# Decay rows of the float32 score tiles issued from GpSimd's queue, and another issue order

## The chip, the cores and the metric

The kernel runs on one core of a Trainium2 chip. The metric is the device time of one execution in microseconds (us). Three runs of the kernel before took 1042.11, 1043.04 and 1045.21 us; their median, 1043.04 us, is the time that the change is measured against. One further execution was profiled; it took 1040.97 us, and the first and the last instruction in its trace are 1039.0 us apart (its span).

## The reference: what is computed

Eight batches of eight heads, each with 576 positions of 64 values, go through causal attention with a decay, and the result (4608 tokens of 512 values) through two matrix products with a cosine between them.

```python
scores = scale * np.matmul(q, k.transpose(0, 1, 3, 2))
log_f = np.log(np.clip(f, 0.0001, 1.0))
cum = np.cumsum(log_f, axis=-1)
decay = cum[:, :, :, None] - cum[:, :, None, :]
scores = np.where(causal, -1000000000.0, scores + decay)
...                                   # softmax over the last axis, then times v
h = x @ w_in
g = h * np.cos(h)
return (g @ w_out).astype(np.float32)
```

The decay is a difference of two numbers, one of the row and one of the column. The kernel lays `cum` as an extra row beside the 64 rows of q and another beside those of k (with constants as partners), so the matmul that makes the scores adds the decay as well.

## The kernel before, in words

**Tiling.** Heads are taken in pairs, so there are 32 pairs, four to a batch. Each head's scores are five blocks of 128 rows, cut at the diagonal, in three PSUM tiles: one with 576 columns (`pa2`), one with 448 and 64, and one with 320 and 192 (both `pa1`). The first four pairs (`N32 = 4`) run `attention32`: scores in float32 (line 697, two products of 288 columns for the 576), exponentials on ScalarE (line 715), transposes on TensorE (line 668) with evacuations (lines 656, 657), products with v (line 742), a division by the sums (755, 756, 758), transposes (765) and a split into two float16 halves (769, 771). Pairs 4 to 7 still make float32 scores (line 865) from the same kind of tile, but go on like the rest: softmax (879, 884, 889, 892), halves of the probabilities (901, 905), a transpose by DMA (910), products with v (934). Pairs 8 to 31 use split scores (867, 868).

**The float32 tiles.** Pairs 0 to 7 (`NQ = 8`) use four tiles `Q`, one for each head of two pairs in turn. `load32` fills one: 64 partitions of q and k by a 288 KB transfer (line 636, on SyncE's queue, SP), and two decay rows of 576 numbers (2.2 KB each, line 640), one to partition 64 and one to partition 65. The rows come from SBUF (`cm`, shown as `vv`, since it lies in that buffer) in the first batch and from a copy in DRAM (`cum_d`) in the second. A tile's rows can only be written when the score matmuls of the tile's user before are done. Pair 0 (`NACT = 1`) issues its four rows from ScalarE's queue.

**The weights.** Both weight matrices come in as 64-bit words. VectorE makes float32 of them (483, 487, 491), ScalarE takes a bound by a sum of squares (502), a largest value over all partitions is found by `allmax` (a diagonal tile `dg` made on VectorE at line 434 or on GpSimd at line 438, a matmul at line 441, a maximum at line 443), GpSimd makes a power of two of it (424, 425), and the weights are split in float16 halves (512, 519, or 516 and 517 on GpSimd). A raw block waits for its place in a ring of three (`h`) or eight (`g`).

**The MoE part.** `gemm1` (line 964) and `gemm2` (line 1010), each by three float16 products for one float32 product; the cosine stage lies between them (970 to 994).

**The order.** Every piece of work is an operation with a number, recorded in program order. The string `ORDER` lists these numbers in the order in which all engines' instructions are issued; each engine works through its own part of it in sequence, and waits where its next instruction's inputs are not there. An "a" behind a number takes the operation's other form (a piece of work that VectorE and GpSimd can both do, say). "+44" behind a number puts 44 filler matmuls (line 1077, 448 columns, results never read) on TensorE ahead of that operation.

```python
for pads, fill, fn in seq:
    for _ in range(pads):
        T.matmul(fill(), ones, mask[:, 0:PAD], start=True, stop=True)
    fn()
```

Of the kernel before, what the change touches and what calls it, by code (L numbers as in the profile page):

```python
# [43 lines left out]
N32, NQ, NACT = 4, 8, 1  # L44
# [27 lines left out]
796 586a 786 601 604 813 787 597 797 818 542 799 617 605 798 819 602 773 598 800 820 618+1 801 607 814 802 606 949 821 619 803 948 825 804  # L72
620 774 621 599 822 837 805 622 826 623 608 624 806 658 600 625 807 641 662+1 827 626 828 838 659 642 808 678 627 839 643 609 676+1 823 628
679 644 663 629 664+2 809 677 630 645 810 829 631 646 811 830 660 840 831 632 832 610 672 665 661 633 841 877+1 634 673 647 674+1 878 635
648a 824 833 611 834 858+3 933 836 842 636 714 879 843 637 859 649 692 638 844 835 650 675 845 639 698 612 893 651 984 860 640 865 652 693
666 880 861 862 667 613 699 653 846 614 668 694 654 700 847 848 655 669 863 889 657 670 680 681 715 986 710 947 656 682 864 695 881 866 1438
701 867 683 868 882 869 696 883 895 870 671a 871 884 697 885 926 712 872 886 873 887 684 874 849 1148 890 876 875 896 702 902 853 891 927
914 897 903 850 716 898 711 1022 851 945 904 915 713 899 726 916 905 888 717 906 718 917 730 727 907 728 731 985 908 918 719 1026 900 919
1029 854a 969 909 703 920 901 729 724 910 921 911 922 720 913 912 950 970 923 686 685a 951 924 971 972 957 1027a 704 958 925 959 952 721 687
973 953 725 954 974 1031 960 955 975 732 1021 994 961 928 956 962 1082 963 733 964 965 976 987 966 977 734 995 1083 968 1032 978 705 996 967  # L80
979 997 735 941 929 1006 998 980 1445 999 688 1007 1023 1008 1000 988 1009 689 1010 1229 989 1028 1001 706 690 1011 990 1002 1012 691 991
1013 1003 1030 1014 946 1273 722 707 1015 992 723a 1004 1016 942 981 993 1017 736 934 943 737 1230a 1084 982 708 983 709 1085 1234a 1231
1033 1005 1018 1034 935 936a 1235 1040 1019 1086 1020 1052 1041 937 1068 1274a 1053 938 1054 1042 1055 1278a 1275 1070 1035 1276 1956 1043
1232 1036 1037 1069 939 1072 940 1056 1038 1071 1044 1074 1073 1045 1446 1046 1024 1057 1058 1279 1124 1314 1075 1047 1277 1076 1233 1270
1077 1126 1125 1048 1059 1039 1078 1122 1957 1025 1064 1049 1127 1060 1120 1061 1065 1050 1079 1243 1121 1062 1123 1236 1271 1128 1140 1080
1066 1129 1255 1100 1318 1315 1081 1051 1130 1134 1320a 1237 1238 1131 1101 1102 1244 1132 1087 1239 1319a 1256 1317 1245 1240 1103 1063
1257 1141 1246 1133a 1241 1287 1258 1138 1242 1259 1316 1288 1104 1247 1289 1280 1248 1290 1260 1249 1136 1250 1281 1135 1251 1291 1252 1139
1108 1292 1447a 1137 1665 1254 1142 1261 1143 1110 1262 1282 1109 1283 1263 1284 1253 1112 1144 1293 1584 1264 1272 1355 1299 1358 1265 1106
1266 1111 1145 1294 1113 1151 1285 1300 1107 1114 1155 1115 1359a 1105 1153 1156 1152 1286 1149 1154 1301 1116 1363 1360 1321 1458 1302 1448
1117 1088 1267 1295 1150 1296 1118 1094 1364 1298 1297 1303 1157 1268 1089 1304 1305 1449 1306 1158 1146 1090 1307 1147a 1159 1308 1340 1399  # L90
1309 1095 1341 1342 1322 1311 1269 1323 1119 1328 1091 1403 1329 1400 1324 1361 1160 1310 1096 1404a 1092 1312 1325 1450 1326 1313 1330 1207
# [150 lines left out]
T_DGE = 0.5  # L242
# [79 lines left out]
def fox_moe_kernel(ctx: ExitStack, tc: tile.TileContext, qkT, vp, fT, w1, w2, out):  # L322
    nc = tc.nc
    V, A, G, T = nc.vector, nc.scalar, nc.gpsimd, nc.tensor
    dma = nc.sync.dma_start
# [37 lines left out]
    ks = slice(64, 64 + S)  # L363
# [744 lines left out]
```

## Time and profile before

| | |
|---|---|
| median of three runs | 1043.04 us |
| the profiled execution | 1040.97 us |
| its span | 1039.0 us |
| TensorE busy in the span | 1027.0 us (99%) |
| VectorE, ScalarE, GpSimd busy | 774.9, 789.5, 294.8 us |
| granted TensorE clock | 1.000 |
| filler matmuls | 99 |
| decay-row transfers issued by SP, by ScalarE | 28, 4 |

A busy TensorE here is one that executes matmuls, the fillers among them. The engines' shares over the whole span hide that the kernel has two stages: about the first 100 us, in which weights are read and converted and the first pairs are worked off, and the rest, in which the two matrix products dominate. The prediction reads them apart.

### The profile page before, as it was taken

What the parts mean: (1) busy time and instruction counts of PE and PEld (TensorE: products, weight loads), DVE (VectorE), ACT (ScalarE), POOL (GpSimd) and SP (SyncE); (2) the same over time, 40 slices, a digit from 0 to 9 for tenths busy, and PEclk for the clock granted to TensorE, in tenths of its full rate; (3) what the DMA queues carried; (4) which work ended last, traced back from release to release, by engine and by line L of the source; (5) the groups of instructions that cost most, each with busy time, mean ns of one, the idle gap of its engine ahead of it and who ended that gap; (6) DMA issues with size and microseconds to landing.
All of it is one profiled execution on the core that took longest, in us unless ns stands there. A gap on an engine that the chain in (4) does not pass through costs nothing. (4 is left out here: it accounts for less than half of the span.)

```text
span 1039.0 us, 23384 instructions
## 1 busy us (share of the span) xinstructions
PE 1027.0 (99%) x8915; PEld 831.6 (80%) x8916; DVE 774.9 (75%) x1710; ACT 789.5 (76%) x1711; POOL 294.8 (28%) x381
## 2 busy tenths in 40 slices
PE   8999999999999999999999999999999999999998
PEld 4788777778888877888778877888778877888787
DVE  8999998778678676787877688586877967663531
ACT  5999999788768797898877789686878877753431
POOL 3223213432341343332332424233141313300110
PEclk9999999999999999999999999999999999999999
DMA  8997525856685757668465766947466583520001
GB/s 261 288 321 200 130 55 128 185 107 162 154 175 147 163 132 163 139 144 183 114 145 135 176 142 159 193 83 164 124 170 136 121 189 56 122 39 16 7 14 34
DMA packets 255920, 144.77 MB, mean 139 GB/s; under 512 B 223736, under 2 KB 231928, under 8 KB 255808
## 3 DMA queue, kind: packets, MB, share of 16 engines
q1 hardware_dynamic: 255680, 143.27, 58.4%
q8 instruction: 70, 1.15, 0.4%
q14 instruction: 42, 0.34, 0.1%
q10 hardware_dynamic: 128, 0.01, 0.0%
HBM read 71.41 MB, written 9.68 MB: 78 GB/s over the span
## 5 line engine op out<-in xcount | busy, mean ns | idle before, releaser
L1010 PE MATMUL hp<-g,W2s 128*128 128x320 f16 (+1 forms) x3072 | 391.8, 286 | 0.2
L964 PE MATMUL hp<-xh,W1s 128*128 128x320 f16 (+1 forms) x2048 | 381.3, 286 | 1.5 <-ACT h L970 1.4
L964 PEld LDWEIGHTS <-W1s 128*128 128x128 f16 x3072 | 295.5, 98 | 78.6 <-issue 1.8
L1010 PEld LDWEIGHTS <-W2s 128*128 128x128 f16 x3072 | 296.3, 98 | 76.1 <-issue 0.6
L964 PE MATMUL hp<-xl,W1s 128*128 128x256 f16 (+1 forms) x1024 | 292.6, 286 | 0.0
L905 DVE SCALAR_TENSOR_TENSOR PS<-pa,ri,PS 128x576 f16<-128x576 f32 (+3 forms) x280 | 146.1, 544 | 57.3 <-ACT PS L901 55.9
L884 ACT ACTIVATE pa<-pa,nb 128x576 f32<-128x576 f32 (+4 forms) x280 | 141.5, 506 | 48.5 <-DVE nb L879 43.1
L901 ACT ACTIVATE PS<-pa,ri 128x576 f16<-128x576 f32 (+3 forms) x280 | 137.7, 531 | 31.1 <-DVE ri L892 27.0
L889 POOL TENSOR_SCALAR ri<-L 128x1 f32<-128x1 f32 (+1 forms) x168 | 53.9, 321 | 352.0 <-ACT pa L884 347.1
L879 DVE CUSTOM_DVE_ANT_0 pa<-pa,mask 128x576 f32<-128x576 f32 (+4 forms) x280 | 134.7, 500 | 24.0 <-PE pa L868 20.4
L970 ACT ACTIVATE h<-hp 128x320 f32<-128x320 f32 (+1 forms) x256 | 100.1, 411 | 36.5 <-PE hp L964 32.8
L994 POOL TENSOR_TENSOR g<-h,g 128x1024 f16<-128x1024 f32 (+1 forms) x32 | 83.5, 2609 | 149.0 <-ACT g L992 147.3
L985 DVE TENSOR_TENSOR h<-h,r 128x1280 f32<-128x1280 f32 (+1 forms) x64 | 89.6, 1399 | 34.4 <-ACT r L983 33.9
L983 ACT ACTIVATE r<-r,halfpi,m_inv 128x1280 f32<-128x1280 f32 (+1 forms) x64 | 86.2, 1348 | 31.2 <-DVE r L981 29.0
L981 DVE SCALAR_TENSOR_TENSOR r<-r,m_b,h 128x1280 f32<-128x1280 int32 (+1 forms) x64 | 93.6, 1462 | 1.1
L867 PE MATMUL pa<-Q 128*128 128x288 f32 (+4 forms) x288 | 90.4, 327 | 1.2 <-DVE PS L905 0.7
L979 DVE TENSOR_SCALAR r<-h,m_a 128x1280 int32<-128x1280 f32 (+1 forms) x64 | 54.9, 858 | 44.9 <-ACT h L970 43.0
L992 ACT CAST g<-h 128x1280 f16<-128x1280 f32 (+1 forms) x64 | 73.8, 1154 | 10.6 <-DVE h L985 10.4
L934 PEld LDWEIGHTS <-vv 128*64 128x64 f16 x1512 | 68.6, 110 | 10.3 <-issue 9.5
L868 PE MATMUL pa<-Q 68*128 68x288 f32 (+4 forms) x288 | 76.6, 304 | 0.0
L934 PE MATMUL pa<-pt,vv 128*64 128x256 f16 (+2 forms) x1512 | 76.6, 254 | 0.0
L1016 ACT ACTIVATE ot<-hp,m_o 128x320 f32<-128x320 f32 (+1 forms) x64 | 32.2, 503 | 47.6 <-PE hp L1010 36.2
(127 smaller groups left out, 1182.5 us busy)
## 6 DMA issues: line engine op xcount, KB each, us to landing
stage<-in_dram SPq DMA_DIRECT2D x48, 576.0 KB
stage<-in_dram SPq DMA_DIRECT2D x32, 320.0 KB
v<-in_dram SPq DMA_DIRECT2D x32, 320.0 KB
h<-in_dram SPq DMA_DIRECT2D x16, 512.0 KB
g<-in_dram SPq DMA_DIRECT2D x16, 512.0 KB
Q<-Q SPq DMA_DIRECT2D x48, 144.0 KB
out_dram<-ot SPq DMA_DIRECT2D x32, 160.0 KB
Q<-in_dram SPq DMA_DIRECT2D x16, 288.0 KB
```

The costliest lines, as they stand in the source:

```text
L867: T.matmul(c, hi[:, 0, isl], hi[:, 1, d], start=True, stop=False)
L879: op("DVE", c_dve(w) + 0.008, lambda view=view, ib=ib, o=o, w=w, mk=mk, c=c: V.tensor_tensor_reduce(out=view(ib, o, w), in0=view(ib, o, w) ...
L884: op("ACT", c_act(w, True, 2), lambda view=view, ib=ib, o=o, w=w, c=c: A.activation(view(ib, o, w), view(ib, o, w), AF.Exp, bias=nb.get()[ ...
L901: op("ACT", c_act(w, True, 1), lambda view=view, ib=ib, o=o, w=w, c=c, out_=out_: A.activation(out_(0), view(ib, o, w), AF.Copy, scale=ri. ...
L905: op("DVE", c_dve(w) + 0.06, lambda view=view, ib=ib, o=o, w=w, c=c, out_=out_: V.scalar_tensor_tensor(out_(1), view(ib, o, w), ri.get()[: ...
L934: T.matmul(d, vv.get()[:, jb, hd, kv], m, start=first and x == 0, stop=last and x == 2)
L964: T.matmul(hp.get()[:, 0:w_], WS_[1][:, at(1, 4 * c + cb), w, fs], x.get(), start=(n == 0), stop=(n == 11))
L970: op("ACT", c_act(w_, True), lambda hp=hp, k=k: A.activation(h.get()[:, k, 0:w_], hp.get()[:, 0:w_], AF.Copy, scale=float(2.0 ** -24)), re ...
L981: op("DVE", c_dve(N) + 0.045, lambda: V.scalar_tensor_tensor(fl(r), fl(r).bitcast(I32), b1.get()[:, c:c + 1], fl(h), op0=ALU.mult, op1=ALU ...
L983: op("ACT", c_act(N, aps=2), lambda: A.activation(fl(r), fl(r), AF.Sin, scale=inv.get()[:, c:c + 1], bias=halfpi), reads=[inv], writes=[r] ...
L985: op("DVE", c_dve(N), lambda: V.tensor_tensor(fl(h), fl(h), fl(r), op=ALU.mult), reads=[r], writes=hk, prio=pr)
L1010: T.matmul(po.get()[:, 0:w_], WS_[2][:, at(2, 4 * c + k), w, msl], gh.get()[:, i, k, 0:w_], start=(n == 0), stop=(n == 47))
```

## The change

The decay rows of pairs 1 to 7 (28 transfers) are issued by GpSimd in place of SP; pair 0's stay with ScalarE. The string `ORDER` is another from its first line on, and with it the choice of forms ("a" stands 104 times, before 118 times) and the fillers (110, before 99).

```diff
 ORDER = """
-0 50 60 55 70 25 1 2 4 51 27 52 26 72 61 71 53 62 54 63 3 65 11 56 192 57 95 64 100 6 58 125 7a 170 33+44 28 34 35 40+1 66 37 29 36 67 12
+0 11 50 55 60 95 25 1 2 4 26 125 51 3 52 124 6 7 27 192 56 53 57 54 58 12 65 70 61 72 59 62 96 71 170 63 97 64 33+53 175 100 40 9 34 105 66
 ...
         for k, r in ((1, 64), (0, 65)):
-            op(*(("SP", T_DGE) if n >= NACT else ("ACT", 0.35)), lambda k=k, r=r: (dma if n >= NACT else A.dma_start)(t[r:r + 1, k, ks], src()),
+            op(*(("POOL", 1.0) if n >= NACT else ("ACT", 0.35)), lambda k=k, r=r: (G.dma_start if n >= NACT else A.dma_start)(t[r:r + 1, k, ks], src()),
                reads=[CF if b > 0 else cm], writes=[q.part(1 + k)], prio=pr, size=DMC // 4)
```

The numbers beside an engine's name (0.5 as `T_DGE`, 0.35, 1.0) are planning costs in us; the order in the string was laid out by them, and nothing in the running program reads them.

**GpSimd, after its opening memsets.** Here stand GpSimd's next twelve rows before: the decay's small remainder (line 462), then the steps of `allmax` (409 clamps a maximum, 438 makes the diagonal tile), of the scale (424, 425) and of the sums (755).

```order
L462 TENSOR_TENSOR g<-vv,g 64x576
L409 TENSOR_SCALAR m_w<-m_w 128x1
L424 TENSOR_SCALAR s_109<-u_w 128x1
L425 TENSOR_SCALAR r_110<-u_w 128x1
L755 TENSOR_SCALAR ri<-L 128x2x3
L755 TENSOR_SCALAR ri<-L 128x2x2
L409 TENSOR_SCALAR vm_427<-vm_427 128x1
L438 TENSOR_SCALAR dg<-eye,vm_427 128x128
L409 TENSOR_SCALAR m_w<-m_w 128x1
L424 TENSOR_SCALAR vs<-vu 128x1
L425 TENSOR_SCALAR vr<-vu 128x1
L438 TENSOR_SCALAR dg<-eye,m_w 128x128
```

And the same stretch of the changed kernel.

```order
L640 DMA Q<-vv 1x16x36 x3
L409 TENSOR_SCALAR m_w<-m_w 128x1
L640 DMA Q<-vv 1x16x36 x2
L424 TENSOR_SCALAR s_109<-u_w 128x1
L425 TENSOR_SCALAR r_110<-u_w 128x1
L755 TENSOR_SCALAR ri<-L 128x2x2
L640 DMA Q<-vv 1x16x36
L755 TENSOR_SCALAR ri<-L 128x2x3
L640 DMA Q<-vv 1x16x36
L409 TENSOR_SCALAR vm_435<-vm_435 128x1
L640 DMA Q<-vv 1x16x36
L438 TENSOR_SCALAR dg<-eye,vm_435 128x128
```

Decay-row transfers now stand between the small steps; line 462 is gone from GpSimd. One row further on, and in two later places, transfers stand again just ahead of a line 409 or 438.

**SP, from its first transfer.** The transfer of f (`vv`), raw weights (`h`, `g`), v for a bound (`stage`), q and k (`Q`) and, before, decay rows.

```order
L451 DMA vv<-in_dram 64x576
L493 DMA h<-in_dram 128x1024 x3
L636 DMA Q<-in_dram 64x2x576 x2
L493 DMA h<-in_dram 128x1024
L582 DMA stage<-in_dram 128x640
L640 DMA Q<-vv 1x16x36
L493 DMA g<-in_dram 128x1024 x2
L640 DMA Q<-vv 1x16x36
```

The same queue in the changed kernel.

```order
L451 DMA vv<-in_dram 64x576
L582 DMA stage<-in_dram 128x640
L493 DMA h<-in_dram 128x1024 x3
L493 DMA g<-in_dram 128x1024
L636 DMA Q<-in_dram 64x2x576
L493 DMA h<-in_dram 128x1024
L636 DMA Q<-in_dram 64x2x576
L493 DMA h<-in_dram 128x1024 x2
```

A `stage` and a `g` transfer moved ahead of the first `Q`, and a fourth `h`, which waits for its place in the ring, moved between the first and the second `Q`.

**VectorE, behind the running sum of the decay (line 455).** A piece of the difference:

```order
 L483 TENSOR_SCALAR W1s<-h 128x512
 L487 SCALAR_TENSOR_TENSOR W1s<-h,W1s 128x512
+L458 CAST g<-vv 64x576
+L460 TENSOR_TENSOR g<-vv,g 64x576
 L483 TENSOR_SCALAR W1s<-h 128x512
 L491 SCALAR_TENSOR_TENSOR W1s<-h,W1s 128x512
```

Line 458 came six rows later before, and line 460 takes the work of GpSimd's line 462.

More of the change, by code (lines that the diff above doesn't have):

```diff
@@ L72 @@
[L72 to L79, printed above, removed]
@@ new lines @@
+318 248 285 295 378 212 152 543 221 197 313 544 259 305 236 504 153 226 345 286 270 249 260 237 545a 154 203 250 291 235 319 204 446 109 113
+254 227 255 222 356 292 546 325 261 357 320 238 362 340 547 256 293 740 262 263 326 266 265 548 503 393+1 264 296 257 306 267 287 239 294
+268 297 240 300 327 359 314 329 445 328 298 230 322 307 358 242 371 335 394 321 308 315 241 333 377 299 271 386+1 404 502 395 549 372 309
+485 301 330 397 1443 302 381 334 288 387 396 303 316 323 332a 304 382 453+1 317 410 289 411 383 412a 460 228 331 388 324 454 739 384 360 461
@@ new lines @@
+770 479 581 771 795 593 582 571 591+1 588 782 594 583 572 603 592 584 783 772+1 615 595 616 604 784 796 617a 540 785 596 786 812 541 773 787
+597 601 797 799 798 542 818 1067 813 800 598 585 618 605+1 602 774 586a 599 819 801 820 619 607+2 802 620 814 621 622 803 623 658 821 624
+606 600 608 625 662 804 822 626 641 805 823 825 642 627 806 837 826 659 807 628 678 663 985 808 838 629 827 839 949 643 660 809 630 679 828
+894 810 676+1 631 644 811 948 840 632 829 664 609 645 830 661 831 657 633 646 672 677 610 832 892 841 877+1 944 665 842 647 984 634 673
@@ new lines @@
+1002 1013 707 1003 1014 737a 690 1015 942 691 1004 992 1016 981 946 1017 1084 943 982 1230 993 1085 708 1234a 709 1021 1033 1232 1018 1005
+1034 983 1040 1019 1086 1020 1052 1041 1072 1274 1445 1446 935 936 1235 1035 1279a 1068 1053 1270 1042 1276 1054 1043 1278 1055 1070 1036
+1073 1037 1314 1038 1233 1056 1074 1956 1044 1275 1069 1045 1231 1071 1057 1046 1047 937 1048 1124 1075 938 1447a 1039 939 1076 940 1064
+1024 1077 1125 1120 1271 1049 1025 1078 1051 1122 1058 1957 1126 1059 1079 1065 1060 1121 1236 1123 1050 1087 1127 1061 1140 1080 1277 1128
@@ new lines @@
+1129 1100 1141 1237 1130 1101 1062 1066 1063 1238 1243 1131 1255 1287 1244 1102 1132 1256 1239 1081a 1257 1288 1134 1315 1240 1245 1289 1290
+1316 1319 1103 1455 1246 1320a 1241 1138 1247 1242 1258 1104 1248 1358 1259 1249 1280 1291 1260 1250 1133a 1136 1281 1135 1139 1251 1282
+1252 1108 1137 1261 1254 1262 1142 1292 1263 1283 1112 1143 1293 1110 1264 1113 1284 1109 1265 1144 1253 1318 1106 1317 1266 1299 1107 1145
+1111 1151 1285 1399 1294 1155 1114 1359 1115 1152 1153 1360 1363a 1156 1286 1116 1267 1300 1301 1448 1154 1149 1449 1146 1117 1321 1302 1272
@@ new lines @@
+1464a 1499 1378 1379 1461 1177 1414 1099 1371 1162a 1380 1415 1391 1178 1381 1416 1383 1392 1356 1393 1165 1382 1417 2182 1394 1406 1425
+1407 1352 1500a 1426 1408 1427 1166 1179 1395 1409 1353 1504a 1204 1354 1428 1410 1411 1169 1418 1505a 1419 1463 1420 1501 1429 1460 1170
+1430 1180 1502 2101 1462 1421 1171 1543 1422 1746 1423 1357 1396 1431 1412 1432 1433 1434 1172 1424 1456 1435 1167 1472 1484 1473 1465 1485
+1205 1486 1544 1466 1168 1474 1467 1457 1181 1503 1436 1475 1468 1549a 1397 1487 1182 1398 1476 1488 1477 1478 1469 1489 1470 1547 1183 1173
@@ new lines @@
+1585 1559 1831 1590 1553 1796a 1554 1560 1200 1794 1588 1555 1591 1561 1225 1562 1795a 1571 1563 1611 1556 1875 1760 1586 1793 1753 1564
+1761 1592 1623 1754 1565 1572 1226 1617 1566 1755 1762 1568 1593 1612 1763 1756 1594 1764 1227 1765 1613 1573 1228 1595 1574 1618 1567 1575
+1772 1614 1835 1832 1834 1596 1792 1619 1576 1836a 1577 1757 1766 1624 1578 1620 1615 1767 1579 1773 1837a 1580 1597 1605 1774 1775 1816
+1599 1817 1787 1758 1818 1958 1616 1606 1776 1759 1819 1777 1778 1768 1779 1769 1607 1780 1820 1770 1781 1804 1782 1598 1797 1783 1621 1581
@@ new lines @@
+1682 1908 1664a 1928 1909 1910 1688 1973 1911 1943 1914 1912 1944 1930 1945 1683 1946 1931 2017a 1929 2020 1932 2021 1689 1933 1978 2019
+1974 1684 1934 1685 1935 1668 1947 1936 2022a 1948 1937 1915 1949 1693 1938 1950 2060 1951 1939 1690 1669 1694 1952 1940 1674 1953 1675 1698
+1676 1982 1941 1695 1983 1984 1677 1969 1989 2001 1678 1990 2018 1699 1691 2061a 1991 1970 2002 1992 1971 2003 1985 2062 1700 2004 2065a
+1986 2064 1987 2063 1993 1988 2005 1994 2013 1995 2006 1679 2066a 1996 1696 1997 2007 1697 1701 2008 1998 2009 2000 2014 2010 1999 2023 2011
@@ new lines @@
+3072 3073 3082 2736 3075 3074 3101 3048 3083 3120 2745 3084 2752 3121 3122 3085 3123 2738 3102 3124 2753 3086 3125 3103 2740 3087 3104 2766
+2741 2739 2746 2754 3299 3105 2747 3106 3091 3338 2767 2756 3301 2755 3107 2748 3300 3341 3049 3126 2758 3426 3088 2757 2749 2759 3127 3132
+3089 3128 2750 3129 3090 2768 2760 3130 2761 2770 2769 3133 2751 3108 2771 2762 3311 3344 3342a 3134 3304 3109 2999 3140 3110 2763 3111
+3346a 3343 3323 3136 3324 2764 3000 3305 3141 3325 2772 3347 3326 3327 3312 3382 3306 3138 3345 3001 3313 2765 3385 3112 3307 3137 3002 3314
@@ new lines @@
+3644 3645 3831 3840 3646 3856 3674 3900a 3841 3832 3647 3663 4113 3670 3905a 3842 3862 3675 3901 3648 3833 3824 3834 3904a 3825 3680 3826
+3671 3827 3835 3681 3664 3843 3672 3903 3685 3943 3836 3844 3676 3837 3845 3846 3839 3838 3847 3884 3848 3665 3865 3885 3686 3866 3677 3849
+3867 3691 3850 3666 3868 3678 3851 3687 3869 3886 3872 3870 3682 3944a 3887 3871 3888 3947 3873 3896 3889 3683 3948a 3890 3874 3684 3875
+3946 3876 3945 3688 3949a 3897 3902 3891 3898 3984 3892 3719 3893 3877 4028 3878 3894 3879 3880 3692 3881 3852 3689 3720 3883 3882 3906 3853
```

199 lines of the change are left out of this document (82 added, 117 removed), and 51 rows, old and new, of the table ORDER.

## The prediction

> **What bounds the kernel now.** I read the page's first part, then the table of stretches, then TensorE's waits, then the timelines of the first 100 us.
>
> ```profile
> span 1039.0 us, 23384 instructions
> PE 1027.0 (99%) x8915; PEld 831.6 (80%) x8916; DVE 774.9 (75%) x1710; ACT 789.5 (76%) x1711; POOL 294.8 (28%) x381
> ```
>
> TensorE is idle for 12.0 us in all. So the time is its work, plus its fillers, plus these 12.0. The waits say where they lie:
>
> ```profile
> PE pa L1077 <- POOL ones L346: 2.3, 1, 2.3
> PE hp L964 <- ACT h L970: 1.4, 3, 0.6
> PE hp L668 <- ACT PS L715: 1.1, 1, 1.1
> PE pa L697 <- DMA Q<-in_dram: 0.7, 1, 0.7
> PE pa L867 <- DVE PS L905: 0.7, 2, 0.4
> PE pa L697 <- ACT PS L715: 0.6, 2, 0.3
> PE pa L867 <- DVE xl L942: 0.4, 1, 0.4
> PE pa L697 <- issue: 0.3, 1, 0.3
> PE pa L865 <- DVE ri L892: 0.3, 1, 0.3
> PE hp L765 <- DVE m_w L443: 0.2, 1, 0.2
> 1035.68 0.47 ACT L1016 ACTIVATE ot<-hp,m_o 128x256 f32<-128x256 f32 x1 [3.09 <-PE hp L1010]
> ```
>
> The first row is the start (2.3 us until the tile of ones is there), the last is the end: TensorE is done at about 1035.6 us, and the last evacuation and store take the other 3.4. Neither part's order changes. Between them nine waits make 1.4 + 1.1 + 0.7 + 0.7 + 0.6 + 0.4 + 0.3 + 0.3 + 0.2 = 5.7 us: that is all that any reordering can take from the waits.
>
> The table of stretches (length; busy us of PE, PEld, DVE, ACT, POOL; clock; DMA share; GB/s) shows two stages:
>
> ```profile
> 0.00:12.70 12.70, 10.40 (x45) 5.03 (x46) 9.80 (x17) 4.79 (x8) 6.12 (x24) 1.00 0.74 221
> 12.70:97.00 84.30, 81.19 (x548) 66.52 (x547) 81.10 (x235) 75.06 (x221) 23.01 (x47) 1.00 0.94 279
> 25.00:50.00 25.00, 23.67 (x154) 18.68 (x154) 23.74 (x65) 22.93 (x70) 5.87 (x12) 1.00 1.03 294
> 97.00:150.00 53.00, 52.65 (x412) 39.85 (x412) 51.71 (x117) 50.76 (x109) 10.85 (x17) 1.00 0.48 111
> 150.00:300.00 150.00, 149.28 (x1301) 118.21 (x1299) 115.38 (x269) 119.86 (x260) 53.72 (x73) 1.00 0.66 150
> 300.00:1000.00 700.00, 697.92 (x6316) 572.64 (x6315) 504.92 (x1066) 528.88 (x1102) 198.16 (x221) 1.00 0.57 127
> ```
>
> Up to 97 us VectorE is busy for 81.1 of 84.3 us, the DMA engines for 94%, and TensorE's 81.2 are partly fillers. GpSimd has 61 us to spare there. From 97 us TensorE is the bound (99.3 to 99.7%), VectorE falls to 77% and then 72%.
>
> The fillers:
>
> ```profile
> L1077 PEld LDWEIGHTS <-ones x99: 95/98/153, 2.3 to 146.0; 128*128 128x128 bf16 x99
> 2.29 10.56 PE L1077 MATMUL pa<-mask,ones 128*128 128x448 bf16 x44 [2.29 <-POOL ones L346]
> 12.69 2.11 PE L697 MATMUL pa<-Q 66*128 66x448 f32 x8
> 32.01 1.68 PE L1077 MATMUL hp<-mask,ones 128*128 128x448 bf16 x8
> 33.52 0.60 PE L668 MATMUL hp<-eyef,PS 128*128 128x128 f32 x4
> ```
>
> There are 99, counted here by their weight loads, the last at 146 us. Eight of them from 32.01 to 33.52 us make one 0.189 us. The first 44 end as the first scores start, at 12.69 us, and nothing is waited for there.
>
> **The change part by part.** TensorE's real work is the same matmuls in the same numbers. *Fillers:* 110 for 99. A filler runs whether it is needed or not, so eleven more cost 11 x 0.189 = 2.08 us. Nine of them stand ahead of the first scores, which then start at 12.69 + 9 x 0.189 = 14.4 us. They would cost nothing where TensorE would have waited for something else anyway, at most for the waits of today's first 97 us (1.1 + 0.7 + 0.6 + 0.3 + 0.2 = 2.9 us): the lower end is 0. I take 2.08, since VectorE, which these fillers wait for, gets more to do.
>
> *VectorE's share.* By its order it gains one each of lines 460, 519 and 657 ahead of the first gemm and loses one of 434 (GpSimd's 462, 516 with 517, and 438 change the other way; line 657 comes from ScalarE).
>
> ```profile
> L808 DVE TENSOR_TENSOR Q<-stage,Q x1: 755/755/755, 185.2 to 185.2; 64x576 fp32r<-64x576 f32 x1
> L519 DVE SCALAR_TENSOR_TENSOR W1s<-W1s,s 128x512 f16<-128x512 f32 x13 | 9.7, 743 | 1.0 <-ACT W1s L512 1.0
> L657 DVE COPY pt<-hp 128x384 f32<-128x384 f32 x1 | 0.5, 548 | 0.0
> L434 DVE TENSOR_SCALAR dg<-eye,m_w 128x128 bf16<-128x128 bf16 x2 | 0.5, 248 | 0.1
> L458 DVE CAST g<-vv 64x576 fp32r<-64x576 f32 x1 | 0.4, 447 | 0.0
> L993 DVE TENSOR_TENSOR g<-h,g 128x1280 f16<-128x1280 f32 (+1 forms) x32 | 43.6, 1362 | 8.8 <-ACT g L992 8.8
> L825 DVE SCALAR_TENSOR_TENSOR vv<-v,vs,vv 128x640 f16<-128x640 f32 x22 | 19.5, 895 | 0.7 <-issue 0.7
> ```
>
> Line 460 has no row; line 808 has its shape. 0.755 + 0.743 + 0.548 - 0.248 = 1.8 us more, in a stage where VectorE has 3.2 us idle in 84.3. That is the same lengthening that the fillers fill, so 1.8 and 2.08 are one cost and are not added. Later VectorE also gets nine more of line 993 and six more of 825 and gives up eight of 808: 9 x 1.36 + 6 x 0.90 - 8 x 0.76 = 11.6 us. Hidden: VectorE idles for 35 us of the stretch 150 to 300 and for 195 us of 300 to 1000, under a TensorE at 99.5%. Without that cover it would be all 11.6.
>
> *The moved transfers.* Issuing on SP took:
>
> ```profile
> L640 SPq DMA_DIRECT2D Q<-cum_d x16: 232/332/634, 52.0 to 173.7; - x16
> L640 SPq DMA_DIRECT2D Q<-vv x12: 501/514/601, 11.1 to 58.9; - x12
> 24.34 0.63 POOL L424 TENSOR_SCALAR s<-u_w 128x1 int32<-128x1 int32 x1 [3.78 <-DVE u_w L416]
> 73.03 0.19 POOL L424 TENSOR_SCALAR s<-u_w 128x1 int32<-128x1 int32 x1 [1.76 <-DVE u_w L416]
> L438 POOL TENSOR_SCALAR dg<-eye,vm x7: 626/629/1310, 33.9 to 800.0; 128x128 bf16<-128x128 bf16 x7
> L994 POOL TENSOR_TENSOR g<-h,g 128x1024 f16<-128x1024 f32 (+1 forms) x32 | 83.5, 2609 | 149.0 <-ACT g L992 147.3
> ```
>
> SP gives up 12 x 0.514 + 16 x 0.332 = 11.5 us of issuing over 160 us. That gain reaches TensorE only by earlier transfers, and in 25 to 50 us the engines that carry them are already full (1.03, 294 GB/s): I take 0, with 0.7 us (the one wait on `Q<-in_dram`) as the bound for a gain. What a transfer costs GpSimd no row shows. From below it is GpSimd's shortest instruction, 0.19 us; from above its long one, 2.61. I take 1.0, between SP's 0.51 and L438's longest 1.31, since a transfer is a small instruction like these, and L424's two rows (0.63 and 0.19 us for the same 128x1) show GpSimd's small instructions stretched at times. 28 x 1.0 = 28 us fit in the 61 + 42 us that GpSimd has to spare up to 150 us: cost 0, if none stands ahead of something urgent. Where one does, see the second rival. A transfer that waits for its tile holds the whole queue behind it: the scale (424) and the diagonal tile (438), which TensorE's line 441 waits for.
>
> *SP's new head.* Ahead of the first Q now lie 144 + 320 + 3 x 512 + 512 KB; with Q's 288 that is 2.8 MB, which at the 221 GB/s of the first stretch is there at 12.7 us. TensorE comes to it at 14.4: hidden, with 1.7 us to spare. The second Q stands behind an h that waits for line 502.
>
> ```profile
> 9.24 0.63 ACT L502 ACTIVATE h<-W1s 128x512 bf16<-128x512 f32 x1 [3.98 <-DVE W1s L491]
> 9.99 0.35 SPq L493 DMA_DIRECT2D h<-in_dram  x1
> ```
>
> Lines 458 and 460 now go ahead of that conversion (0.45 + 0.76 = 1.2 us), so this h goes out at 11.2 us; 0.8 MB more at 294 GB/s end at 15.4, and the second head's first scores stand, behind two groups of the first head (2.1 us by the row at 12.69), five fillers and a third group, at 14.4 + 2.1 + 5 x 0.189 + 1.0 = 18.5 us: hidden by 3 us.
>
> *Sum.* 2.08 + 0 + 0 + 0: the profiled execution's 1040.97 (span 1039.0 and 1.97 around it) would become 1043.05. The median of the runs lies 2.07 us above that execution, and the change is the same on it: 1043.04 + 2.08 = **1045.1 us**, +0.2%. About 0.3% (3.1 us) is what a measurement of this kernel can tell from no change, so this forecast counts as the same.
>
> **The rivals.** *Faster: the new order leaves no waits (18%).* SP, free of 28 issues, sends raw weights earlier, the fillers sit where TensorE waits today, and all nine waits go: 1045.1 - 5.7 = 1039.4. For it: 0.7 us is a wait on a transfer. Against: it needs nearly all, 5.2 of 5.7, and five of the nine wait for ScalarE or VectorE in the stage where both are full, or for line 970 later.
>
> *Slower: GpSimd's transfers hold up `allmax` (21%).* L424 takes 0.19 or 0.63 us, L438 0.63 or 1.31 on the same shape: GpSimd is held up by up to 0.68 us an instruction while VectorE is busy, which it is for 96% of this stage. Seven transfers stand ahead of the diagonal tiles or clamps of four maxima. If each takes 0.68 more than laid out and TensorE, which works in order, stands at line 441 for it: 7 x 0.68 = 4.8, giving 1049.9. It decides from 1.0 us in all, 0.15 for each. Against: ahead of L424's two rows GpSimd had waited 3.78 and 1.76 us for its input, and in such gaps a transfer of 1 us fits. The Trainium skill ("SBUF — State Buffer", section "SBUF: two separate sides") states the same mechanism as a rule: a DMA from GpSimd's queue has its descriptors written by GpSimd's cores, and these are locked out while VectorE runs in a two-port mode; it gives 620 ns alone and 3100 ns under a VectorE copy. By these figures an estimate is 7 x 2.48 = 17.4 us, which would make 1062.5. No run here shows it yet; the two lengths of L438 point the same way, at a quarter of the size.
>
> *Slower: the early loads are late (18%).* The 44 fillers may hide that Q's load itself ends close to 12.7 us. Then 832 KB more ahead of it (2.8 us at 294 GB/s) put the first scores 1.1 us behind the fillers, and the 1.2 us of lines 458 and 460 ahead of the first weights add to the stage: 1045.1 + 2.3 = 1047.4. For it: DMA 94%. Against: only 0.74 in the first stretch.
>
> **How the numbers follow.** My forecast has 43% and reaches from 1043.0 (fillers free) to 1046.1. Faster by over 0.3% (below 1039.9): 18%; within 0.3%: 43%; slower (above 1046.2): 21 + 18 = 39%. The range, 1039.5 to 1051.0, holds half of the faster case and the two slower ones but for the long end of GpSimd's transfers.
>
> **What would show it.** In the profile after: 110 fillers; the first scores at 14.4 us and no wait on Q there; the transfers in a queue of their own, about 1 us each on GpSimd; TensorE's waits between start and end still 4 to 8 us; first gemm (line 964) at 98 to 100 us, where it now starts at 96.65. I am wrong if a wait on line 441, 438 or a `Q` row over 1 us appears, or if the waits fall below 1 us.
>
> ```profile
> 96.65 0.43 PE L964 MATMUL hp<-xh,W1s 128*128 128x320 f16 x2
> ```

## The result, and the profile after

The changed kernel took 1060.03 us (median of 1058.22, 1062.00, 1061.83 and 1051.27), the kernel before 1042.57 us beside it (1043.04, 1042.11, 1045.21, 1041.34). The two medians give a ratio of 1.017; the ratio estimated from all executions is 1.0146, with a 95% interval of 1.0115 to 1.0176. The changed kernel is slower by 1.5%, and 1060 us lies outside the range that was given. The mean granted TensorE clock of the four executions was 0.987, 0.984, 0.985 and 0.993, where the execution profiled before had 1.00. Ratios in this document leave out an execution that stands over 1.5% above the fastest one of its kernel (below, one of 1069.60 us and one of 1055.16 us).

The page of the changed kernel (the execution of 1058.22 us): the span, TensorE's busy time, and TensorE's granted clock in 40 slices of 26 us.

```profile
span 1056.5 us, 23401 instructions
PE 1040.4 (98%) x8927; PEld 843.1 (80%) x8927; DVE 783.4 (74%) x1719; ACT 795.1 (75%) x1714; POOL 269.3 (25%) x390
PEclk9979899999999999999999999999999999999999
```

The span grew by 17.5 us: TensorE is busy 13.4 us longer, with the same real work, and idle 4.1 us longer. The clock's row has a 7 and an 8 in its third and fifth slice. The table of stretches (length; busy us of PE, PEld, DVE, ACT, POOL; clock; DMA share; GB/s), cut where the clock changes, shows them at full size:

```profile
53.20:56.60 3.40, 2.37 (x12) 1.77 (x13) 2.74 (x13) 2.49 (x8) 2.27 (x5) 1.00 1.02 380
56.60:70.20 13.60, 13.60 (x57) 12.31 (x56) 9.63 (x27) 7.31 (x23) 1.19 (x2) 0.50 0.58 174
...
97.50:100.90 3.40, 1.82 (x14) 1.53 (x14) 3.40 (x8) 2.74 (x7) 2.72 (x5) 1.00 0.63 183
100.90:114.60 13.70, 13.70 (x57) 11.33 (x56) 9.03 (x26) 7.42 (x22) 4.00 (x9) 0.50 0.70 135
```

Twice TensorE ran at half its clock for some 13.65 us. All of it was busy time, so each stretch gave half its length of work: 2 x 6.8 = 13.65 us lost, and (1 - 0.987) x 1056.5 = 13.7 by the mean clock. Just ahead of each stretch TensorE had stood still, as its timeline shows (start, length, what ran; in brackets the idle time before it and what ended it):

```profile
54.23 1.16 PE L697 MATMUL pa<-Q 66*128 66x448 f32 x4 [1.21 <-DMA Q<-in_dram]
...
100.18 0.35 PE L1077 MATMUL pa<-mask,ones 128*128 128x448 bf16 x1 [1.58 <-DVE PS L905]
...
111.85 0.74 PE L964 MATMUL hp<-xh,W1s 128*128 128x320 f16 x2
```

The third row is the first gemm: 111.85 us where it was 96.65, so 15.2 of the 17.5 us are lost ahead of it. TensorE's busy time up to the first gemm, all of it and then its fillers alone (line 1077), before:

```profile
0.00:96.65 96.65, 91.24 (x588) 71.28 (x589) 90.55 (x252) 79.50 (x227) 29.09 (x69) 1.00 0.91 272
0.00:96.65 96.65, 22.65 (x88) 9.31 (x88) 1.00 0.91 272
```

and after:

```profile
0.00:111.85 111.85, 104.67 (x605) 83.19 (x606) 94.84 (x262) 81.01 (x232) 36.32 (x87) 0.89 0.84 244
0.00:111.85 111.85, 24.10 (x101) 10.28 (x101) 0.89 0.84 244
```

Fillers 22.65 to 24.10, real work 68.59 to 80.57, idle 5.41 to 7.18: +1.45, +11.98 and +1.77 make the 15.2. Real work is the same matmuls; it took longer by the clock alone. The last 2.76 us of the second slow stretch lie behind the first gemm (another 1.4 us lost), which leaves 0.9 us for everything later.

Where the two gaps come from, the other queues tell. The first gap waits for the Q load of the second head of pair 2, which SP issued at 38.74 us before (first fence) and at 44.43 us after (second). By then SP had issued one `h`, three `g` and two copies to `cum_d` more than before:

```profile
38.74 0.59 SPq L636 DMA_DIRECT2D Q<-in_dram  x1
```

```profile
44.43 0.55 SPq L636 DMA_DIRECT2D Q<-in_dram  x1
```

The second waits for VectorE to give back the PSUM tile `pa2` (line 905), and in the new order VectorE has two steps of the raw weights ahead of that, one of them 1.26 us long, where the same line took 0.42 us at 86.31 and at 88.98 us (the changed kernel's timeline):

```profile
97.43 0.67 DVE L487 SCALAR_TENSOR_TENSOR W2s<-g,W2s 128x512 int32<-128x512 int32 x1
98.02 1.26 DVE L483 TENSOR_SCALAR W2s<-g 128x512 int32<-128x512 int32 x1
...
99.34 0.79 DVE L905 SCALAR_TENSOR_TENSOR PS<-pa,ri,PS 128x576 f16<-128x576 f32 x1
```

Before, line 905 followed directly on the softmax's line 879 there, and the weights' steps came only behind it, from 92.80 us on:

```profile
90.32 0.14 DVE L879 DVE_READ_ACCUMULATOR2_ANT nb<- 128x1 f32 x1
90.32 1.40 DVE L905 SCALAR_TENSOR_TENSOR PS<-pa,ri,PS 128x576 f16<-128x576 f32 x2
```

That the two steps of the weights make the second gap is read from these timelines; no run moved them.

The moved rows themselves, in the changed kernel's groups (ns min/median/max of one issue on GpSimd):

```profile
L640 POOL DMA_DIRECT2D Q<-cum_d x16: 484/540/712, 54.8 to 162.5; - x16
L640 POOL DMA_DIRECT2D Q<-vv x12: 487/544/725, 6.4 to 56.0; - x12
```

### The profile page after: what moved, and what is told of

It reads as the page before. It is cut to its first block, busy times and chain, and to the rows that moved or that the text cites. A ratio compares the mean times of both kernels' runs of the same rounds, so it can differ in the third digit from the quotient of the medians.

```text
span 1056.5 us, 23401 instructions
## 1 busy us (share of the span) xinstructions
PE 1040.4 (98%) x8927; PEld 843.1 (80%) x8927; DVE 783.4 (74%) x1719; ACT 795.1 (75%) x1714; POOL 269.3 (25%) x390
## 4 chain that ended last, share of the span: by engine, by line
PE 78%; ACT 9%; DVE 6%; DMA 4%; issue 3%; POOL 1%; SPq 0%; DVEq 0%; ACTq 0%; POOLq 0%
PE hp L1010 32%; PE hp L964 28%; PE pa L934 5%; PE pa L867 3%; PE pa L868 3%; PE hp L742 2%; DMA Q<-in_dram 2%; PE pa L697 2%; DMA pt<-PS 2%; PE pa L865 1%; ACT r L983 1%; ACT L983 1%; DVE h L985 1%; ACT pa L884 1%; ACT PS L901 1%
## 5 line engine op out<-in xcount | busy, mean ns | idle before, releaser
L905 DVE SCALAR_TENSOR_TENSOR PS<-pa,ri,PS 128x576 f16<-128x576 f32 (+2 forms) x280 | 145.2, 544 | 51.0 <-ACT PS L901 49.9
L979 DVE TENSOR_SCALAR r<-h,m_a 128x1280 int32<-128x1280 f32 (+1 forms) x64 | 52.5, 820 | 50.1 <-ACT h L970 48.6
L994 POOL TENSOR_TENSOR g<-h,g 128x1280 f16<-128x1280 f32 (+1 forms) x23 | 57.5, 2501 | 118.0 <-ACT g L992 117.5
L934 PEld LDWEIGHTS <-vv 128*64 128x64 f16 x1512 | 68.6, 110 | 11.1 <-issue 10.3
```

Source lines behind the costliest of these rows:

```text
L905: op("DVE", c_dve(w) + 0.06, lambda view=view, ib=ib, o=o, w=w, c=c, out_=out_: V.scalar_tensor_tensor(out_(1), view(ib, o, w), ri.get()[: ...
L934: T.matmul(d, vv.get()[:, jb, hd, kv], m, start=first and x == 0, stop=last and x == 2)
```

## The experiments

**Theory "clock":** the new order leaves two gaps in TensorE's work, 1.2 and 1.6 us, and each makes the granted clock fall to half for 13.65 us (6.8 us of work). **Rivals:** "queue" (the rows on GpSimd's queue cost the time) and "late" (late loads cost their own waits, and the clock is a side effect). The kernel before ran beside each group of experiments, 61 executions in all. 17 of them had a mean clock of 0.998 or less, so it has a fall now and then too; the other 44 had a median of 1041.3 us. Below, "full clock" means executions above 0.998. The experiments ran in four groups on four chips: e1 to e4, e5 to e8, e9 to e11, and e12. The kernel before took 1041.08, 1042.33, 1041.22 and 1039.58 us at full clock in these groups (medians), so kernels of different groups can only be compared by what they take above it.

**Both gaps filled** (e1). 318 is the score group that waits at 53 us, 407 the last piece of work ahead of the wait at 98.6 us.

```diff
-318 ... 407
+318+6 ... 407+8
```

> The changed kernel with 14 more fillers, 6 ahead of the scores that wait 1.21 us for their Q rows at 53 us and 8 ahead of the last turn before the 1.58 us wait at 98.6 us. They take the place of idle time: 14 x 0.19 = 2.7 us of fillers where 2.8 us were idle. Theory 'clock' (these two gaps made the granted clock fall to 0.50 for 13.5 us each, 13.6 us lost in all): no stretch at 0.50 any more at 56 and 101 us, granted clock of 0.998 or more, time 1058.2 - 13.6 = 1044.6 us (1043 to 1047). Rival 'queue' (the moved rows on GpSimd's queue cost the time, the clock falls for a reason of its own): the two stretches at 0.50 stay, 1056 to 1062 us. Rival 'late' (the loads are late, each gap costs itself alone): 1058 to 1062 us, as a filled gap is no shorter.

Measured: 1046.73 us (1044.69, 1047.10, 1046.37 at full clock; 1049.67 at 0.995), ratio 1.0063 [1.0043, 1.0083]. The profiled execution has no slow stretch. Its table up to the first gemm, and its fillers:

```profile
0.00:100.27 100.27, 95.72 (x619) 74.08 (x620) 93.53 (x259) 80.20 (x230) 36.42 (x87) 1.00 0.90 267
0.00:100.27 100.27, 26.82 (x115) 11.55 (x115) 1.00 0.90 267
```

Real work is 68.90 us again (68.59 before), idle time 4.55. Fourteen more fillers, matmuls whose results are never read, took the kernel from 17.5 us above the kernel before (medians, 1060.03 and 1042.57) to 5.6 us (1046.73 and 1041.16). "Queue" and "late" fall as explanations of the larger part. What is left at full clock is 5.3 us (1046.37 and 1041.08).

**The order alone (e2), the queue alone (e3).** The changed kernel with its rows in SP's queue (the edit below), and the kernel before with its rows in GpSimd's (the same two lines the other way round).

```diff
-            op(*(("POOL", 1.0) if n >= NACT else ("ACT", 0.35)), lambda k=k, r=r: (G.dma_start if n >= NACT else A.dma_start)(t[r:r + 1, k, ks], src()),
+            op(*(("SP", T_DGE) if n >= NACT else ("ACT", 0.35)), lambda k=k, r=r: (dma if n >= NACT else A.dma_start)(t[r:r + 1, k, ks], src()),
```

> The changed kernel's order and fillers with the 28 rows back in SyncE's queue: the order alone. Theory 'clock', in which the gaps come from the new order (a Q load issued 5.7 us later on SyncE, a score tile freed late at 98.6 us): the gaps stay, and since SyncE also has 28 more issues of about 0.5 us, loads are later still; at least two falls of the clock, 0.985 or lower, 1056 to 1066 us. Rival 'queue': back at 1042 to 1046 us with a clock of 1.00. Rival 'late': 1045 to 1050 us, clock 1.00.

> The kernel before with its own order and fillers, the 28 rows in GpSimd's queue: the queue alone. Theory 'clock': the rows cost 28 x 0.54 us in GpSimd's slack and SyncE is freed of 11.5 us, so no gap over 1.1 us opens before 115 us: clock 1.00, 1041 to 1045 us. Rival 'queue': 1050 to 1062 us, with waits for Q rows or behind them on GpSimd.

The order alone: 1052.52 us (1048.98 to 1062.42), ratio 1.0124 [1.0073, 1.0176], clock 0.993, 1.000, 0.994, 0.987. Both gaps are there again, with the rows in SP's queue:

```profile
54.92 1.40 PE L697 MATMUL pa<-Q 66*128 66x448 f32 x4 [1.08 <-DMA Q<-in_dram]
...
100.89 0.35 PE L1077 MATMUL pa<-mask,ones 128*128 128x448 bf16 x1 [1.34 <-DVE PS L905]
```

The first made a fall, the second did not in this execution, so "at least two" was too many. The queue alone: 1044.73 us (1043.09 to 1047.54), ratio 1.0037 [1.0023, 1.0051]; three of six executions had a fall. In the profiled one it came at the head, where the scores waited for a decay row of pair 0, which ScalarE issues in both kernels (timeline, and the table of stretches):

```profile
13.70 2.18 PE L697 MATMUL pa<-Q 66*128 66x448 f32 x8 [1.18 <-DMA Q<-vv]
```

```profile
16.10:26.20 10.10, 10.10 (x27) 6.72 (x27) 7.70 (x26) 4.05 (x14) 1.04 (x2) 0.50 0.92 296
```

At full clock its median is 1043.96 us (three executions) against 1041.08 beside it, so in the old order the queue costs some 3 us; where they arise is not shown. "Clock" expected no gap of over 1.1 us here, which was wrong. By the medians the order alone stands 11.4 us above the kernel before and the queue alone 3.6 us, where the whole change stands 17.5 us above it: the order makes most of the loss.

**The kernel before without its 55 later fillers** (e4; it leaves out nothing but these).

```diff
-40+1 ... 85+1 ... 78+1 ... 73+1 ... 31+1 ... 38+2 ... 158+3 ... 45+2 ... 131+6 ...
+40 ... 85 ... 78 ... 73 ... 31 ... 38 ... 158 ... 45 ... 131 ...
```

> The kernel before without its 55 fillers behind the first 44 (work left out that no result uses: 55 x 0.19 = 10.4 us of TensorE). Theory 'clock': the places of the fillers between 15 and 42 us become gaps of 1 to 2.5 us, some of them beside the 1.09 us gap at 22 us; the granted clock falls to 0.50 at least once and up to three times for some 13.5 us, each 6.8 us: 1049 to 1063 us, clock 0.980 to 0.994. Rival 'fillers only cost their own time' (the reading in the prediction): clock 1.00, 1033 to 1043 us.

Measured: 1050.41 us, 1042.81 to 1069.60, all eight executions with a fall (clock 0.966 to 0.993). The ratio is 1.0057 [1.0019, 1.0095]. In the profiled execution (1048.26 us, clock 0.987) gaps of 1.29 and 1.97 us stand ahead of, and across the start of, a slow stretch of 27.3 us, from 24.8 to 52.1:

```profile
22.99 0.98 PE L668 MATMUL hp<-eyef,PS 128*128 128x128 f32 x7 [1.29 <-ACT PS L715]
25.94 5.88 PE L697 MATMUL pa<-Q 66*128 66x448 f32 x12 [1.97 <-DMA Q<-in_dram]
```

With 10.4 us of work less the kernel is slower. Less (1 - clock) x span its executions take 1033.3 to 1037.5 us, some 6 us below the kernel before: the work did get shorter, and the clock took more than that. That the fillers only cost their own time is refuted.

**Fewer fillers, placed in these waits** (e7). 22 in place of 55.

```diff
-40+1 85+1 78+1 73+1 31+1 38+2 158+3 45+2 131+6 (and 37 more, all over)
+78+2 158+4 45+7 131+9
```

> The kernel before with 22 fillers behind the first 44 in place of 55, put where the one without any waited longest (0.54, 0.80, 1.29 and 1.97 us, between 18 and 26 us). 33 x 0.19 = 6.2 us of TensorE less. Theory 'clock': no gap over 1.1 us is left, clock 1.00, and between 1041 - 6.2 = 1035 us (if nothing else binds there) and 1041 us (if the early stage is bound by another engine and the fillers only stood in its waits). Rival 'the number of fillers keeps the clock up, not the lack of gaps': falls of the clock as without any, 1045 to 1053 us.

Measured: 1052.77 us (1049.33 to 1054.85), ratio 1.0100 [1.0063, 1.0137], clock 0.982 to 0.990. A miss: the four gaps are closed or shorter, but a new one opened behind them, and the clock fell after it (and once more near 94 us):

```profile
32.17 1.19 PE L697 MATMUL pa<-Q 66*128 66x320 f32 x4 [2.28 <-issue]
```

The kernel before has twelve fillers around this place, which this one lacks. The experiment doesn't tell the number of fillers from the lack of gaps; it shows that a gap moves when another is closed.

**One gap filled (e5); one gap's cause removed (e11).** First only 318+6; then no filler at all, but the awaited Q load (310) issued right behind the one before it (243).

```diff
 # one
-318
+318+6
 # two
-243 ... 310
+243 310 ...
```

> The changed kernel with 6 more fillers at the first gap (53 us) alone; the second (98.6 us, 1.58 us) stays open. Theory 'clock': one fall in most runs, none at 56 us, one near 101 us, 6.8 us: 1046.4 (the median with both gaps filled) + 6.8 = 1053 us where it falls, about 1046 where the gap is split between two windows; clock 0.993. Rival 'the first gap alone sets it' (the second fall is an after-effect of the first): no fall, 1045 to 1047 us.

> The changed kernel with one load moved: the Q load of the second head of pair 2, for which the scores wait 1.21 us at 53 us, is issued on SyncE right behind the Q load before it (at about 37 us instead of 44.4 us). No filler is added. Theory 'clock': the first gap goes with its cause, so no fall at 56 us and one at 101 us in most runs: 1053 us with it, 1046 us where the second gap is split between two windows, as with the first gap filled (median 1052.8 us). If something else held the scores at 53 us: the gap stays, 1058 to 1060 us.

Measured: 1052.77 us (1045.81 to 1058.38; full clock in three of ten executions, median 1047.3, the others 1053.4) and 1052.42 us (1044.37 to 1053.77; full clock in two of nine, the others 1053.0). In both profiled executions TensorE waits for under 0.5 us at 53 us and no fall follows there; one comes behind the second gap (96.70 to 110.36 us) or within it (91.87 to 108.93). So the late Q load made the first gap, each fall comes without the other too (here the second, in the order alone the first), and an execution with a fall takes 6 to 7 us more.

**44 fillers at the head in place of 53** (e6), both gaps filled.

```diff
-33+53
+33+44
```

> The changed kernel with both gaps filled and 44 fillers at the head in place of 53. If the nine cost their own time (the prediction's step): 9 x 0.19 = 1.7 us less than the 1046.4 us of the one with 53, 1044.7 us, first scores at 12.7 us. If the first Q rows land late (in the changed kernel's trace the scores waited 0.69 us for them until 14.7 us): the same time or more, a wait on Q of 1 to 2 us ahead of the first scores, and with over 1.1 us of it a fall of the granted clock near 15 us in some runs (6.8 us): 1046 to 1053 us.

Measured: 1047.25 us (1045.04 to 1057.44). At full clock (six of ten) the median is 1046.25 us, 3.9 above the kernel before in its group; with 53 fillers (e1, three executions) it is 1046.37 us, 5.3 above. The difference, 1.4 us, is near the 1.7 that nine fillers take, but executions at full clock differ by up to 2.9 us here: whether the nine cost their own time in this order is not settled. The profiled execution fell at 38.6 us, behind another gap. There TensorE waits for the diagonal tile (first fence), and on GpSimd a moved decay row stands between the clamp of line 409 and that tile, which itself took 1.77 us where it took 0.67 in the changed kernel (second fence):

```profile
36.98 0.22 PE L441 MATMUL hp<-dg,ones 128*128 128x128 bf16 x1 [1.24 <-POOL dg L438]
```

```profile
34.22 0.23 POOL L409 TENSOR_SCALAR vm<-vm 128x1 f32<-128x1 f32 x1 [3.05 <-DVE vm L591]
34.42 0.69 POOL L640 DMA_DIRECT2D Q<-vv  x1
35.15 1.77 POOL L438 TENSOR_SCALAR dg<-eye,vm 128x128 bf16<-128x128 bf16 x1
```

**Gaps made on purpose in the dense stage** (e8), 15 of them between 229 and 897 us. The lines lie 3 to 5 further on in this kernel.

```diff
+            if gap:
+                T.matmul(fill(), ones, mask[:, 0:PAD], start=True, stop=True)
+                for i in range(gap):
+                    V.tensor_copy(gapt, fill()[:, 0:448])
+                T.matmul(fill(), ones, gapt, start=True, stop=True)
             fn()
```

> The kernel before with 15 gaps made on purpose in the dense stage (250 to 900 us): ahead of 15 groups of the first gemm TensorE writes a filler, VectorE copies it one, two or three times (0.55 us each, so some 0.9, 1.45 and 2.0 us of waiting) and TensorE reads the copy; five of each. Waits of 5 x (0.9 + 1.45 + 2.0) = 22 us and 30 x 0.19 = 6 us of fillers in any case: 1041 + 28 = 1069 us. Theory 'clock', with windows of 3.41 us that fall to half rate from about 1.1 us of idle: none after the short gaps, 4 of 5 after the middle and 4 or 5 of 5 after the long ones, each 13.65 us at 0.50 (6.8 us lost): 1069 + 8 or 9 x 6.8 = 1123 to 1130 us, clock 0.94 to 0.95. Rival 'only the first 115 us are touchy' (load, transfers or a cold start): no fall, 1069 us.

Measured: 1079.00 and 1074.43 us, ratio 1.0333 [1.0282, 1.0384], clock 0.989 and 0.995. Less (1 - clock) x span that is 1067.1 and 1069.1 us, about the 1069 that the waits alone were to make. The theory's number was a miss: three falls from the 15 gaps (and one at 15 us, where the first scores waited 1.34 us), and each lasted 3.41 us, not 13.65. The gaps came out at 0.7 to 0.9, about 1.4, and 2.0 to 2.9 us. Five rows of the table of stretches, to be read for the length, PE's busy time and, third from the end, the clock:

```profile
441.90:445.30 3.40, 2.03 (x18) 1.52 (x16) 2.82 (x5) 2.05 (x7) 2.10 (x4) 1.00 0.54 144
479.40:482.80 3.40, 1.37 (x10) 0.87 (x9) 2.67 (x7) 1.36 (x6) 0.00 (x0) 1.00 0.46 140
482.80:486.20 3.40, 3.40 (x18) 2.26 (x16) 1.60 (x3) 3.35 (x5) 0.00 (x0) 0.50 0.90 167
759.30:762.70 3.40, 2.18 (x16) 1.40 (x15) 3.40 (x5) 3.37 (x6) 3.32 (x2) 1.00 0.08 32
762.70:766.10 3.40, 1.68 (x13) 1.17 (x13) 3.23 (x5) 2.65 (x6) 0.36 (x1) 1.00 0.77 145
```

1.37 us of idle made no fall, 2.03 did, and the longest gap, 2.94 us, which these windows cut into 1.22 and 1.72, did not. "Only the first 115 us are touchy" falls too.

**Dense work behind a gap** (e12). First gap filled, second open, 30 fillers behind the group that follows it.

```diff
-318 ... 494
+318+6 ... 494+30
```

> The changed kernel with the first gap filled (6 fillers), the second left open, and 30 fillers right behind the group that follows the second gap: 5.7 us of dense bf16 matmuls at full clock, up to 11 at half, where float32 matmuls stood. Theory 'the kind of work in the slow windows sets when the clock comes back' (13.65 us among float32 matmuls, 3.41 in the dense stage so far): if the clock falls near 98 us, it comes back after one or two windows (3.41 or 6.83 us). Rival 'a fall before the first gemm lasts four windows whatever runs': 13.65 us. The 30 fillers cost up to 5.7 us: 1046.4 + 5.7 + 1.7 or 3.4 = 1054 to 1056 us by the first, 1059 us by the second.

Measured: 1051.95 and 1052.79 us, ratio 1.0118 [1.0083, 1.0153]. The clock fell at 95.30 us and was back at 98.71, 3.41 us later, where the three other profiled executions that fell behind this gap took 13.65, 13.65 and 17.07 us:

```profile
95.30:98.70 3.40, 3.40 (x10) 1.54 (x9) 2.88 (x10) 2.73 (x10) 1.07 (x3) 0.50 0.61 93
98.70:102.10 3.40, 3.40 (x20) 1.74 (x18) 1.06 (x2) 0.00 (x0) 0.00 (x0) 1.00 1.03 236
```

That speaks for the kind of work and against a fixed length, in one profiled execution. The times lie 2 us below the expected 1054 to 1056, and so does the kernel before in this group (1039.58 us). As a remedy it is too dear: 30 fillers cost up to 5.7 us, and 5.1 us of loss is saved.

**The kernel before with its gaps filled**, with 44 fillers at the head (e9) and with 53 (e10).

```diff
-33+44 ... 45+2 ... 131+6
+33+44 ... 45+7 ... 131+8      # the other: 33+53
```

> The kernel before with 7 more fillers in the two places where TensorE waits longest: 5 more in the 1.09 us wait at 22 us (7 in all), 2 more in the 0.69 us wait at 25 us. 7 x 0.19 = 1.3 us of fillers where 1.8 us are idle. Theory 'clock': the same time at full clock (1041 us), and fewer executions with a fall than the kernel before had (9 of 32); those that stay begin near 15 us, where the first scores come late. Rival 'fillers cost their own time': 1042.3 us at full clock.

> The same with 53 fillers at the head in place of 44, which covers first Q rows that land up to 1.7 us late. Theory 'clock': no fall, or at most one execution in ten, so that all runs stand within 1.5 us of each other; if the first Q rows land at 12.7 us in most executions, the nine fillers cost 1.7 us (1042.7 us); if they land later in most, nothing (1041 us). Rival 'the early falls have nothing to do with the head': as many falls as with 44.

Measured: 1041.42 us (1039.39 to 1055.16), ratio 0.9995 [0.9964, 1.0027], five of twelve executions with a fall; and 1043.01 us (1040.79 to 1044.26), ratio 0.9990 [0.9971, 1.0009], no fall in twelve. The first missed its expectation: five of twelve is no fewer than the nine of 26 of the kernel before beside it, so the two gaps at 22 and 25 us were not what made those falls. With 53 fillers the kernel is no faster than before but steady: no execution stands more than 3.5 us above the best (1.5 were expected). At full clock it takes 1043.0 us, against 1040.3 with 44 and 1041.2 before, so at this place nine fillers do cost their 1.7 us or somewhat more. That the falls they prevent begin at the head is argued; no profiled execution of these two had one. No version beat the kernel before by more than its interval.

## Why the prediction was wrong

**The step that failed** is the first one: "So the time is its work, plus its fillers, plus these 12.0." It takes TensorE's work as a fixed number of microseconds, an idle microsecond as one microsecond lost, and a filler as a cost ("A filler runs whether it is needed or not"). The runs show that a gap of 1.2 us costs 1.2 + 6.8 us where the clock falls after it, and that fillers in a gap can save that. The tables of the kernel before had a clock of 1.00 in every row; it was read and not asked what kept it there. The sum lacked the term "2 falls x 6.8 = 13.65 us", which is most of the 17.5 us.

**Without that term the sum comes near.** The four executions of the changed kernel less (1 - clock) x span give 1044.5, 1045.0, 1045.9 and 1043.9 us; the forecast was 1045.1. This takes off too much where TensorE would have waited anyway: the queue alone comes out at 1039.9 to 1041.0 us that way in its three executions with a fall, and took 1043.1 to 1044.3 in those without. With both gaps filled the changed kernel stands 5.3 us above the kernel before at full clock, where the sum had 2.08, and the first gemm starts at 100.27 us, forecast 98 to 100.

**Its 2.08 us have the right sign; size and origin stay open.** They were put on eleven fillers. Taking nine away at the head saved 1.4 us against the kernel before of its group in the new order, within the scatter, and adding nine there cost 2.7 us in the old order (1043.0 for 1040.3). VectorE's work ahead of the first gemm grew from 90.55 to 93.53 us, 3.0 where 1.8 was forecast, and that stage by 3.6 us, with VectorE busy for 93% of it. That VectorE sets the pace there is argued from these rows; no run tested it alone.

**The moved transfers.** 0.54 us each, where 1.0 was taken. In the new order the runs do not contradict "cost 0": less (1 - clock) x span the order alone takes 1045.0 to 1049.0 us, and with the moved rows 1043.9 to 1045.9. In the old order the queue cost some 3 us at full clock.

**SP's new head.** "Hidden, with 1.7 us to spare" was wrong in the profiled execution: the first scores stood at 14.70 us after 0.69 us of waiting for Q, forecast 14.4 and none. In the five other profiled executions of the new order with 53 fillers at the head the first scores did not wait. Here they came only 0.3 us later than forecast, since the 53 fillers had ended at 14.01 us. That moment is no fixed one: in every profiled execution the first 8 to 16 fillers took 0.35 to 0.37 us each, until 5.0 to 8.0 us after the start, and the later ones 0.19. So the first scores of these six stood between 13.81 and 15.12 us.

**The rivals.** "The early loads are late" (18%) did happen: at the head in one of six profiled executions, with 0.69 us of waiting where it named 1.1, and at 53 us, where it named nothing. The waits are a small part of what they cost; the sign that the prediction named for being wrong, a `Q` row over 1 us, is the 1.21 us row. "GpSimd's transfers hold up `allmax`" (21%) did not in the changed kernel, where the longest wait on line 441 is 0.3 us and not for GpSimd. But in two variants of the new order line 441 waited 1.24 us (44 fillers at the head) and 1.02 us (dense work behind a gap) for a diagonal tile behind a moved row, and in the first of them the clock fell after it. So this path is there in the new order, and the row's 0.69 us are a part of it. The estimate from the Trainium skill ("SBUF — State Buffer", section "SBUF: two separate sides"), 1062.5 us, comes near the measured time by accident: its 3.1 us were taken as time that a transfer holds GpSimd beside a busy VectorE, and there the longest of the changed kernel's rows is 0.73 us (from issue to landing they took 1.6 to 7.2 us). "Faster: no waits" failed, as TensorE's waits between start and end rose from 5.7 to 10.3 us; the forecast was 4 to 8.

## What to carry to other kernels

Before changing an order, look at TensorE's gaps, not only at their sum: a gap of over a microsecond in a stage of small float32 matmuls can cost several times its length, by the clock. Fillers that stand in such a wait cost next to nothing (with both gaps filled, 2.7 us more of fillers and 2.6 us less of idle time than in the changed kernel) and hold the clock up; where TensorE would not have waited they cost their time. A reordering has to take them along to where the new waits are. Where the mean clock differs between executions of one kernel, compare them at equal clock first, and read the table of stretches where the clock's row dips.

## What the runs showed of the hardware

**The clock changes on a grid of 3.413 us.** Rows of 0.2 us of the changed kernel around the four changes:

```profile
56.40:56.60 0.20, 0.20 (x3) 0.18 (x2) 0.20 (x2) 0.20 (x1) 0.13 (x1) 0.95 1.18 425
...
70.20:70.40 0.20, 0.20 (x4) 0.20 (x3) 0.20 (x1) 0.00 (x0) 0.00 (x0) 0.92 1.30 246
...
100.80:101.00 0.20, 0.20 (x2) 0.14 (x2) 0.20 (x1) 0.20 (x1) 0.00 (x0) 0.88 0.04 12
...
114.60:114.80 0.20, 0.20 (x3) 0.16 (x2) 0.00 (x0) 0.20 (x2) 0.00 (x0) 0.98 1.58 112
```

A share of 0.50 in each row puts the changes at 56.58, 70.23, 100.95 and 114.61 us. The slow stretches are 13.65 us = 4 x 3.413 long, and the falls 44.37 us = 13 x 3.413 apart. In the run with gaps made on purpose the falls at 15.20, 332.64, 482.83 and 629.60 us lie 93, 137 and 180 such steps from the first. That suggests that whether a gap makes the clock fall depends also on how the grid cuts it, and the grid lies differently in each execution: the changed kernel had a loss of about two falls in three executions and one in the fourth. The Trainium skill ("TensorE: Matmul & The Clock Gate", section "Part 1: The HAM clock gate (the "warmup" mystery)") gives free-running windows of 3413 ns; the rows agree to the hundredth.

**How much idle time it takes.** The steps of that grid are called windows here. In the first 120 us windows with 1.04 to 2.28 us of idle stood ahead of every fall (twelve windows in ten profiled executions), none with 0.80 us or less did, and three with 1.14, 1.14 and 1.23 us were followed by no fall. In the dense stage with gaps made on purpose 1.65, 2.03 and 2.03 us were, 1.44 us or less were not, and 1.64 and 1.69 us were not (windows of 3.413 us here; the rows of the experiment are 3.40 us long). So a third of a window could be enough among float32 matmuls, about half among float16 ones, and there is no sharp limit by idle time alone. The same page (section "HAM oscillation — how this bites in real kernels") has a rule against gaps over some 3.4 us. Here windows with 1.0 to 2.3 us of idle were enough, so for this kernel the rule is too mild.

**How long it lasts.** Among the float32 matmuls of the first 115 us the clock came back after 3 to 8 windows in ten falls, though TensorE was busy for nearly all of that time, and after one window in one (at 94.5 us in the kernel with 22 fillers); in the dense stage after one, three times of three, and after one behind the gap that was followed by 30 bf16 fillers. What counts as activity, so that a fully busy window of float32 matmuls is mostly too little, stays open.
